# Hash-masked attention with an MLP behind it: values loaded a head at a time over all partitions, one store a unit, first score steps over three pairs of banks

## The chip, the cores and the metric

One Trainium2 chip; the kernel runs on one core of it. The metric is the device time of one execution in microseconds (us), as a median over runs; a profile is of one further execution.

## The reference, cut to what matters

```python
def _attn_ref(q, k, v, proj):            # q, k, v: (4, 8, 768, 64) f32; proj: (64, 6)
    q_bits = (np.einsum('bhsd,dk->bhsk', q, proj) > 0).astype(np.int64)
    k_bits = (np.einsum('bhsd,dk->bhsk', k, proj) > 0).astype(np.int64)
    powers = 2 ** np.arange(n_bits)
    q_bucket = np.sum(q_bits * powers, axis=-1)
    k_bucket = np.sum(k_bits * powers, axis=-1)
    mask = q_bucket[:, :, :, None] == k_bucket[:, :, None, :]
    scores = np.where(mask, scale * np.matmul(q, k.transpose(0, 1, 3, 2)), -1e9)
    attn = softmax(scores)
    return np.matmul(attn, v)

def _moe_ref(x, g_ln, w_ch1, w_ch2):     # x: (4, 768, 512), the heads side by side
    xn = (x - mu) / np.sqrt(var + 1e-06) * g_ln
    ch = np.maximum(xn @ w_ch1, 0.0) @ w_ch2      # 512 -> 2048 -> 512
    return x + ch
```

Each query attends to the keys whose six sign bits equal its own. The result, with the eight heads side by side, goes through a layer norm and a two-layer MLP, and is added to it.

## The kernel before, in words

The work is cut into 12 **units** u of 256 query rows, three for each batch b. A unit has six **score steps** s = 6u + 3g + kp: g is a group of four heads, kp a pair of key blocks (256 keys). The whole program is a list of words, `ORDER`, each `operation.engine.arguments` (v VectorE, a ScalarE, p GpSimd, s SyncE, t TensorE); the kernel goes through it and issues one operation after the other. Each engine executes its own words in that order and waits at a word until its inputs are there and its output's buffer is free. A transfer's words stand in the queue of the engine that issues them in the same way. So a word that waits holds every later word of its engine.

The words that matter here, with lines of the kernel before:

- **Loads of q and k.** `lx` (batch 0) loads the slices of some kp for four heads, `LX` (L417, other batches) 768 KB at once, into one of four buffers X. `gx` is a memset that claims such a buffer ahead of the load.
- **Turning.** `tn`, `tu` (L234) transpose 32x32 blocks on VectorE; `ca`, `CA` (L237 to 245) cast to bf16, as `qb` and `kb`.
- **Hash.** `ha` and `hc` (batch 0) and `hm` multiply by `proj` on TensorE; `bh`, `bc`, `bt` make bits of +0.5 and -0.5 on VectorE. In batch 0 `sl`, `bi` spread `hc`'s bits; in the others `mw` and `mr` (`G<-Bd`, L452) send them through DRAM. The result G lies so that the product of two G blocks is the mask, added to the scores in the same bank.
- **Values.** `lv` loads values into `vn` (two buffers of four heads each), `cv` (L381) casts them into `vaug` (values and a column of ones), two heads a word; `su`, `sp` or `sq`, and `sc` (L411) make their sum over keys, `vsB`.
- **Steps.** `S` (L476) is 24 matmuls into two pairs of PSUM banks (8 with G, 16 with q and k); `E` (L482) is the exponential on ScalarE, one activation of 128x1024 for each pair; `A` (L501) is 16 matmuls of E with the values into `acc`, which sums over the three steps of a group.
- **End of a unit.** `na`, `nb` divide by the row's sum into x; `nc`, `ce` make the layer norm's statistics and the centred rows; `rs` the inverse deviation on GpSimd; `fl` transposes by DMA (for unit 0 `ft` and `fc` do it on TensorE).
- **MLP.** `F` (L558, p = 0 to 7, 16 matmuls each) the first product, `R` (L566, L568) its ReLU, `D` (L574, in quarters, for each of two row tiles) the second product, `Z` (L582) adds x, `O` (L592) stores. `lw1`, `lw2` (L365, L368) load the weights through GpSimd's queue, four pieces each.
- **Dummies.** `warm`, `wm` and `wa` are matmuls on ones whose results are never read; `warm` is the first `NWARM` of them.

PSUM has eight banks: `scA` two, `scB` two, `acc` two, `f1` and `f2` one each. Buffers of one tag are handed out in turn: E has four, X four, vn two.

The first three score steps (`ROT = (2, 1, 0)`) run over three pairs of banks, scA, scB and acc, since no A has begun by then:

```python
tag = ("scA", "scB", "acc")[(2 * ROT.index(s) + h) % 3] if s in ROT else ("scA", "scB")[h]
```

The hash products `hf` of batch 0 lie in f1 and f2 in turn. The rows of a tile are rows of the sequence in the order 24 tt + 6 c + kj (tt = 0 to 31, c = 0 to 3, partition 32 c + tt). In batch 0 the keys are put by `key_order` into the order of a plain load of values, four heads over 128 partitions in one transfer of 768 KB; in the other batches the values are loaded in the order of the keys, by four transfers of 32 partitions each:

```python
if b == 0:
    eng.dma_start(out=vnat(b, hs), in_=v[b, hs : hs + 4].rearrange("h (p kj) d -> p h (kj d)", p=P))
else:
    eng.dma_start(out=vnat(b, hs)[32 * c : 32 * c + 32], in_=v_view[b][c][:, hs : hs + 4])
```

A unit's rows are stored by four transfers of 32 partitions (128 KB) in the same way, the last unit's in 16 smaller ones on SyncE's and ScalarE's queues.

Of the kernel before, what the change touches and what calls it, by code (L numbers as in the profile page):

```python
# [8 lines left out]
F32 = mybir.dt.float32  # L9
# [4 lines left out]
NWARM = 8  # L14

ROT = (2, 1, 0)
# [7 lines left out]
bh.v.0.1.0 tn.v.1.1.1 ca.v.1.1.1 ha.t.1.1.1 cv.p.0.0.0 E.a.1.1 gx.p.1.0.0 LX.s.1.0.0 bh.v.1.1.1 cv.p.0.0.2 S.t.0.2
E.a.0.0 ha.t.1.0.0 tn.v.1.1.0 ha.t.1.1.0 bh.v.1.0.0 S.t.4.2 bh.v.1.1.0 E.a.0.1 ca.p.1.1.0 tn.v.1.0.2 ha.t.1.1.2
bh.v.1.1.2 cv.p.0.4.2 tn.v.0.0.2 lv.s.1.4.3 A.t.1.2 cv.p.0.4.0 E.a.4.0 sq.t.0.0 lw1.p.2 E.a.4.1 lv.s.1.0.3 S.t.3.2
A.t.2.2 lv.s.1.4.0 sc.a.0.0 lw1.p.1 E.a.3.0 tn.v.0.0.1 hc.t.0.0.2 hc.t.0.0.1 bc.v.0.0.1 E.a.3.1 bc.v.0.0.2 sl.t.0.0.1
bi.a.0.0.1 ca.v.0.0.1 tn.v.1.0.1 sl.t.0.0.2 S.t.5.2 ca.p.1.0.1 lv.s.1.4.1 bi.a.0.0.2 E.a.5.0 A.t.0.2 na.v.0.0 nb.v.0.0
nc.v.0.0 sq.t.0.4 E.a.5.1 sc.v.0.4 S.t.8.2 gx.v.1.0.1 E.a.8.0 gx.v.1.1.0 A.t.5.2 A.t.4.2 ca.p.1.0.2 tu.v.1.0.0.0
LX.s.1.0.1 A.t.3.2 E.a.8.1 na.v.0.1 nb.v.0.1 lw1.p.3 S.t.6.2 E.a.6.0 lv.s.1.0.1 nc.v.0.1 ce.v.0.0 hc.t.1.0.2 hc.t.1.0.1  # L30
A.t.8.2 bc.v.1.0.1 E.a.6.1 S.t.7.2 A.t.6.2 bc.v.1.0.2 lv.s.1.4.2 ce.v.0.1 E.a.7.0 pmem.p tu.v.1.0.0.1 rs.p.0 gx.v.1.1.1
sl.t.1.0.1 on.p.1 sl.t.1.0.2 LX.s.1.1.1 bi.v.1.0.2 bi.v.1.0.1 E.a.7.1 lw1.p.0 tu.v.1.0.0.3 ft.t.0.1 ft.t.0.0 fc.v.0.0
LX.s.1.1.0 S.t.9.2 tu.v.1.0.1.2 fc.a.0.1 A.t.7.2 lw2.p.1 lw2.p.0 tu.v.1.0.1.1 lw2.p.3 ca.a.0.0.2 cv.p.1.4.0 F.t.0.4
tu.v.1.0.1.3 E.a.9.0 E.a.9.1 na.v.1.0 F.t.0.3 R.v.0.4 S.t.10.2 R.a.0.3 A.t.9.2 lw2.p.2 E.a.10.1 F.t.0.6 tu.v.1.0.0.2
CA.v.1.0.0 E.a.10.0 nb.v.1.0 nc.v.1.0 R.a.0.6 F.t.0.7 S.t.11.2 E.a.11.0 tu.v.1.0.1.0 E.a.11.1 CA.p.1.0.1 su.p.1.4
hm.t.1.0 bt.v.1.0 A.t.10.2 R.a.0.7 tu.v.1.1.0.2 tu.v.1.1.1.3 tu.v.1.1.1.1 S.t.14.2 tu.v.1.1.0.1 mw.s.1.0 mr.s.1.0.0
F.t.0.2 tu.v.1.1.0.3 R.v.0.2 A.t.11.2 E.a.14.1 na.v.1.1 nb.v.1.1 E.a.14.0 F.t.0.5 tu.v.1.1.1.2 S.t.12.2 R.v.0.5 F.t.0.0
E.a.12.0 nc.v.1.1 R.v.0.0 E.a.12.1 A.t.14.2 F.t.0.1 S.t.13.2 A.t.12.2 R.a.0.1 lv.s.1.0.2 D.t.0.0.0 E.a.13.0 ce.v.1.0
E.a.13.1 D.t.0.0.1 ce.v.1.1 rs.p.1 fl.s.1.1 tu.v.1.1.1.0 fl.s.1.0 tu.v.1.1.0.0 mr.s.1.0.3 S.t.16.2 E.a.16.0 E.a.16.1
LX.s.2.0.0 mr.s.1.0.2 hm.t.1.1 lv.s.1.0.0 bt.v.1.1 CA.p.1.1.0 mr.s.1.0.1 D.t.0.0.2 mw.s.1.1 sp.t.1.4 sc.v.1.4 S.t.15.2  # L40
cv.p.1.4.2 F.t.1.7 R.v.1.7 E.a.15.0 E.a.15.1 cv.p.1.0.0 A.t.13.2 D.t.0.0.3 na.v.2.0 F.t.1.5 CA.a.1.1.1 Z.v.0.0 S.t.17.2
LX.s.2.1.1 E.a.17.1 R.v.1.5 mr.s.1.1.3 su.p.1.0 D.t.0.1.0 F.t.1.2 R.v.1.2 LX.s.2.0.1 mr.s.1.1.1 mr.s.1.1.0 LX.s.3.0.1
D.t.0.1.1 E.a.17.0 S.t.18.2 E.a.18.1 lv.s.2.0.3 mr.s.1.1.2 F.t.1.3 R.v.1.3 D.t.0.1.2 D.t.0.1.3 nb.v.2.0 E.a.18.0
F.t.1.0 lv.s.2.0.0 A.t.15.2 S.t.20.2 E.a.20.0 R.v.1.0 F.t.1.1 R.a.1.1 Z.v.0.1 tu.v.2.0.0.1 A.t.17.2 nc.v.2.0 A.t.16.2
F.t.1.4 cv.p.1.0.2 tu.v.2.0.0.3 E.a.20.1 S.t.19.2 E.a.19.0 na.v.2.1 A.t.20.2 R.v.1.4 nb.v.2.1 nc.v.2.1 ce.v.2.1
lv.s.2.4.1 tu.v.2.0.0.2 D.t.1.0.0 E.a.19.1 fl.s.2.1 F.t.1.6 R.a.1.6 S.t.21.2 D.t.1.0.1 E.a.21.0 E.a.21.1 lv.s.2.4.2
ce.v.2.0 tu.v.2.0.0.0 D.t.1.0.2 D.t.1.0.3 CA.p.2.0.0 tu.v.2.0.1.0 tu.v.2.0.1.1 sp.t.1.0 sc.a.1.0 A.t.18.2 fl.s.2.0
S.t.22.2 E.a.22.1 LX.s.2.1.0 E.a.22.0 tu.v.2.0.1.2 tu.v.2.0.1.3 CA.a.2.0.1 hm.t.2.0 O.s.0.0 lv.s.2.0.1 Z.v.1.0 bt.v.2.0
D.t.1.1.0 S.t.23.2 F.t.2.0 LX.s.3.0.0 E.a.23.1 D.t.1.1.1 lv.s.2.4.3 lv.s.2.4.0 R.a.2.0 E.a.23.0 tu.v.2.1.0.0 lv.s.2.0.2
# [59 lines left out]
def kernel(  # L109
# [16 lines left out]
    P = 128  # L126
# [510 lines left out]
```

## Time and profile before

| what | value |
|---|---|
| runs | 308.54, 305.88, 308.46 us; median 308.46 |
| profiled execution, span | 308.1 us |
| TensorE busy | 297.0 us, 96% of the span |
| ScalarE, VectorE, GpSimd busy | 187.9 (61%), 174.4 (57%), 84.6 us (27%) |
| moved by DMA | 34.32 MB |
| TensorE's first and last matmul | starts at 1.11, last ends at 303.74 us |
| last store landed | 306.4 us |

The profiled execution's span, 308.1 us, lies 0.4 us below the median of the runs and is the yardstick for the working; the time that the runs give is counted as the span and those 0.4 us. A row of a time view gives the start of an instruction, its time, its engine and line, the operation, output and input with partitions and elements, and in brackets the idle time ahead of it with what ended that.

### The profile page before, as it was taken

What the parts mean: (1) busy time and instruction counts of PE and PEld (TensorE: products, weight loads), DVE (VectorE), ACT (ScalarE), POOL (GpSimd) and SP (SyncE); (2) the same over time, 40 slices, a digit from 0 to 9 for tenths busy, and PEclk for the clock granted to TensorE, in tenths of its full rate; (3) what the DMA queues carried; (4) which work ended last, traced back from release to release, by engine and by line L of the source; (5) the groups of instructions that cost most, each with busy time, mean ns of one, the idle gap of its engine ahead of it and who ended that gap; (6) DMA issues with size and microseconds to landing.
All of it is one profiled execution on the core that took longest, in us unless ns stands there. A gap on an engine that the chain in (4) does not pass through costs nothing.

```text
span 308.1 us, 9875 instructions
## 1 busy us (share of the span) xinstructions
PE 297.0 (96%) x4394; PEld 203.9 (66%) x4394; DVE 174.4 (57%) x363; ACT 187.9 (61%) x204; POOL 84.6 (27%) x102
## 2 busy tenths in 40 slices
PE   8898699999999999999999999999999999999994
PEld 4576477567667766856676677676676776676663
DVE  4757777646926956666866434556464335345112
ACT  3687667775786867755657586665755686351220
POOL 3675625626233950141020028301001001001000
PEclk9999779999999999999999999999999999999999
DMA  6999999488594587124032030131010501103032
GB/s 213 358 263 194 296 252 199 69 248 232 118 278 112 135 106 192 46 65 129 2 87 54 9 108 2 40 81 36 10 45 19 102 4 27 43 2 91 30 85 69
DMA packets 31290, 34.32 MB, mean 111 GB/s; under 512 B 15632, under 2 KB 27920, under 8 KB 31248
## 3 DMA queue, kind: packets, MB, share of 16 engines
q1 hardware_dynamic: 26656, 29.24, 37.2%
q0 software_dynamic: 4224, 4.19, 8.4%
q8 instruction: 34, 0.56, 0.8%
q10 hardware_dynamic: 368, 0.26, 0.3%
q14 instruction: 8, 0.07, 0.1%
HBM read 28.12 MB, written 6.88 MB: 114 GB/s over the span
## 4 chain that ended last, share of the span: by engine, by line
PE 86%; DVE 4%; DMA 4%; ACT 3%; SPq 1%; issue 1%; DVEq 0%
PE f L558 27%; PE sc L476 17%; PE acc L501 11%; ACT E L482 3%; DMA X<-in_k_dram 3%; PE hp L431 2%; PE hf L323 1%; DMA xnT<-xc 1%; PE f_60None L574 1%; PE f_11None L574 1%; PE f_31None L574 1%; PE f_71None L574 1%; PE f_50None L574 1%; PE f_21None L574 1%; PE f_20None L574 1%; PE f_101None L574 1%
## 5 line engine op out<-in xcount | busy, mean ns | idle before, releaser
L482 ACT ACTIVATE E<-sc,bias_sb 128x1024 bf16<-128x1024 f32 x144 | 153.5, 1110 | 64.1 <-PE sc L476 64.1
L558 PE MATMUL f<-xnT,w_sb 128*128 128x256 bf16 x768 | 100.6, 275 | 0.2 <-DMA xnT<-xc 0.2
L558 PEld LDWEIGHTS <-w_sb 128*128 128x128 bf16 x768 | 71.9, 98 | 22.1 <-issue 5.2
L568 DVE TENSOR_SCALAR hb<-f 128x512 bf16<-128x512 f32 x48 | 33.0, 688 | 46.9 <-PE f L558 46.3
L574 PEld LDWEIGHTS <-hb 128*128 128x128 bf16 x400 | 36.7, 98 | 33.3 <-issue 4.5
L476 PE MATMUL sc<-qb,kb 32*128 32x256 bf16 x1152 | 53.1, 269 | 0.0
L566 ACT ACTIVATE hb<-f 128x512 bf16<-128x512 f32 x48 | 28.6, 596 | 39.9 <-PE f L558 38.5
L501 PEld LDWEIGHTS <-E 128*128 128x128 bf16 x1152 | 41.8, 98 | 7.4 <-issue 5.1
L501 PE MATMUL acc<-vaug,E 128*128 128x65 bf16 x1152 | 45.7, 195 | 0.0
L476 PE MATMUL sc<-G 6*128 6x256 bf16 (+1 forms) x576 | 43.3, 275 | 1.8 <-ACT E L482 1.7
L536 POOL TENSOR_SCALAR rs<-mv 128x2 f32<-128x2 f32 x12 | 7.8, 654 | 123.2 <-DVE mv L530 122.9
L476 PEld LDWEIGHTS <-kb 32*128 32x128 bf16 x1152 | 30.8, 94 | 1.6
L476 PEld LDWEIGHTS <-G 6*128 6x128 bf16 (+1 forms) x576 | 16.1, 91 | 20.6 <-issue 18.7
L234 DVE STREAM_TRANSPOSE T<-X 128x384 f32<-128x384 f32 x48 | 25.5, 558 | 3.7 <-DMA X<-in_q_dram 3.7
L514 DVE SCALAR_TENSOR_TENSOR y<-vsB,acc 128x520 f32<-128x520 f32 x24 | 16.5, 687 | 18.0 <-PE acc L501 18.0
L531 DVE SCALAR_TENSOR_TENSOR xc<-x,mv,gB 128x512 bf16<-128x512 f32 x24 | 19.1, 798 | 0.9
L381 POOL CAST vaug<-vn 128x768 bf16<-128x768 f32 x16 | 13.5, 859 | 17.8 <-DMA vn<-in_v_dram 11.8
L527 DVE BATCH_NORM_STATS2 st<-x 128x6 f32<-128x256 f32 x48 | 17.6, 411 | 0.3
L389 POOL TENSOR_TENSOR t<-vn 128x768 f32<-128x768 f32 x6 | 10.9, 1814 | 24.7 <-DMA vn<-in_v_dram 24.7
L523 DVE TENSOR_TENSOR x<-y,rc 128x512 f32<-128x512 f32 x24 | 17.2, 715 | 0.8
L243 POOL TENSOR_SCALAR qb<-T 128x1536 bf16<-128x1536 f32 x3 | 12.8, 4267 | 13.5 <-DVE T L234 8.7
L234 DVE STREAM_TRANSPOSE tp<-X 128x256 f32<-128x256 f32 x24 | 9.1, 419 | 3.9 <-DMA X<-in_k_dram 2.8
(115 smaller groups left out, 240.1 us busy)
## 6 DMA issues: line engine op xcount, KB each, us to landing
out_dram<-x SPq DMA_DIRECT2D x44, 128.0 KB
X<-in_k_dram SPq DMA_DIRECT2D x7, 768.0 KB
X<-in_q_dram SPq DMA_DIRECT2D x6, 768.0 KB
vn<-in_v_dram SPq DMA_DIRECT2D x24, 192.0 KB
w_sb<-in_moe_w_ch_dram POOLq DMA_DIRECT2D x8, 512.0 KB, 11.5
vn<-in_v_dram SPq DMA_DIRECT2D x2, 768.0 KB
X<-in_q_dram SPq DMA_DIRECT2D x2, 512.0 KB
Bd<-B SPq DMA_DIRECT2D x6, 96.0 KB
```

Of the source, the lines that this page charges most:

```text
L234: nc.vector.transpose(d[:, j], s[:, j, kj0 : kj0 + n])
L476: nc.tensor.matmul(sc(s, i // 2)[:, i % 2, 256 * kk : 256 * kk + 256], lh, rh, start=(rep == 0), stop=(rep == 2), skip_group_check=True,)
L482: nc.scalar.activation(E(s)[:, heads(h)], sc(s, h), AF.Exp, scale=EXP_SCALE, bias=bias_sb)
L501: nc.tensor.matmul(acc[:, qt, (D + 1) * i : (D + 1) * (i + 1)], E(s)[:, i, 256 * kk + P * qt : 256 * kk + P * qt + P], vaug(u // 3)[:, 4 * ...
L514: nc.vector.scalar_tensor_tensor(yt(u, g), vs, EPS_ROW, made[f"acc{u}{g}"][:, :, :A], op0=AOP.mult, op1=AOP.add,)
L523: nc.vector.tensor_tensor(xo, a[:, :, :, 0:D], rc.to_broadcast([P, 2, 4, D]), op=AOP.mult)
L527: nc.vector.bn_stats(stats(u)[:, qt, g], xt(u)[:, qt, 256 * g : 256 * g + 256])
L531: nc.vector.scalar_tensor_tensor(xc(u)[:, t], xt(u)[:, t], mv(u)[:, t, 0:1], gB, op0=AOP.subtract, op1=AOP.mult,)
L558: nc.tensor.matmul(f1[:, n].rearrange("p (t x) -> p t x", t=2), w1_sb[:, dt, P * nt : P * nt + P], xnT(u)[:, :, dt], start=(dt == 0), stop ...
L566: nc.scalar.activation(hb(u)[:, 2 * p : 2 * p + 2], f1, AF.Relu)
L568: eng.tensor_scalar_max(hb(u)[:, 2 * p : 2 * p + 2], f1, 0.0)
L574: nc.tensor.matmul(f2, hb(u)[:, nt, P * t : P * t + P], w2_sb[:, nt, half(h)], start=(nt == 0), stop=(nt == NNT - 1),)
```

## The change: what it does

Everything is in one step:

- **Values.** `lv` loads one head in one transfer of 192 KB, for all batches: the address list is `c tt (kj d)`, 4 x 32 x 384, onto 128 partitions. `key_order` is dropped: keys of batch 0 stay as loaded. `lv` words: 26 before, 32 after. Some of the `cv` words go to ScalarE and VectorE (10 of 16 stay on GpSimd).
- **Stores.** `O` stores a whole unit in one transfer of 512 KB with the list `c tt (qt d)`, 4 x 32 x 1024; the last unit's goes in three parts. `O` words: 50 on SyncE and 6 on ScalarE before, 14 on SyncE after.
- **Score steps.** The first six (`ROT = (2, 1, 0, 4, 3, 5)`) run over three pairs of banks, and the third pair is now f1 and f2, two tiles of one bank; its E is two activations of 512 in place of one of 1024. The hash products of batch 0 lie mostly in the accumulators' banks.
- **Accumulator.** `acc` is two tiles of one bank; `na` is two instructions in place of one.
- **Small things.** `NWARM` 1 in place of 8; four `wa` words (8 matmuls); `ag` (the statistics' aggregation) a word apart from `ce`; buffers are handed out by an explicit count (`turns`); the load of the activation table moves to a late place.
- **Order.** The whole list of words is remade. It begins with key and query slices and then the eight heads of batch 0's values, one word each.

```diff
-NWARM = 8
-
-ROT = (2, 1, 0)
+NWARM = 1
+
+ROT = (2, 1, 0, 4, 3, 5)
...
-on.p.0 mem.v lp.a tab.a warm.t wm.t.0 wm.t.1 lx.s.0.0.0.1 lx.s.0.1.1.3 pf.v wm.t.2 wm.t.3 lx.s.1.1.0.3 lx.s.0.1.0.1
-lx.s.1.0.0.1 tn.v.0.0.0 ca.a.0.0.0 lx.s.1.0.1.3 lv.s.0.0.4 lv.s.0.4.4 sel.p lx.s.0.0.1.3 p32.p ha.t.0.0.0 wm.t.4 wm.t.5
...
+lx.s.0.1.1.2 mem.v lp.a lx.s.0.0.0.1 wm.t.6 sel.p lx.s.0.1.2.3 wm.t.1 wm.t.0 lx.s.1.0.0.1 wm.t.4 lx.s.0.1.0.1 wm.t.7
+warm.t lx.s.1.1.0.3 pf.v p32.p wm.t.3 lv.s.0.0.2 wm.t.2 tn.v.0.1.1 lv.s.0.0.0 wm.t.5 lv.s.0.0.3 ha.t.0.1.1 ca.p.0.1.1
+tn.v.0.0.0 lv.s.0.4.1 ca.p.0.0.0 ha.t.0.0.0 tn.v.0.1.2 lv.s.0.4.0 bh.v.0.1.1 ca.a.0.1.2 lv.s.0.0.1 bh.v.0.0.0
+ha.t.0.1.2 tn.v.1.0.0 lv.s.0.4.3 tn.v.0.1.0 S.t.1.2 bh.v.0.1.2 ha.t.1.0.0 ca.p.0.1.0 E.a.1.1 ca.v.1.0.0 on.p.0
+lv.s.0.4.2 gx.p.1.0.0 ha.t.0.1.0 E.a.1.0 bh.v.1.0.0 lx.s.0.0.1.3 tn.v.1.1.1 S.t.2.2 LX.s.1.0.0 bh.v.0.1.0 tn.v.1.1.2
...
+D.t.10.1.3 R.a.11.3 F.t.11.5 Z.v.10.1 D.t.11.1.1.1 O.s.10 R.v.11.5 D.t.11.0.0 F.t.11.6 D.t.11.0.1 R.v.11.6
+D.t.11.1.2.1 F.t.11.7 D.t.11.0.2 R.a.11.7 D.t.11.0.3 D.t.11.1.3.1 Z.v.11.0 D.t.11.1.1.0 Z.v.11.1.1 D.t.11.1.2.0
+O.s.11.0 D.t.11.1.3.0 O.s.11.1.1 Z.v.11.1.0 O.s.11.1.0
...
-    v_view = [v[b].rearrange("h (tt c kj) d -> c tt h (kj d)", tt=TT, c=CC) for b in range(B)]
-    out_view = [out[b].rearrange("(tt c u qt) d -> u c tt qt d", tt=TT, c=CC, u=3) for b in range(B)]
+    v_view = [v[b].rearrange("h (tt c kj) d -> h c tt (kj d)", tt=TT, c=CC) for b in range(B)]
+    out_view = [out[b].rearrange("(tt c u qt) d -> u c tt (qt d)", tt=TT, c=CC, u=3) for b in range(B)]
...
+            if tag == "acc":
+                n = turns.get("ps acc", 0)
+                turns["ps acc"] = n + 1
+                tag = f"acc_{n % 2}"
...
-        dst, src = qk(t, 0, g)[:, :, 256 * kp : 256 * kp + 256], tp(g, t, kp)
-        if t == 1:
-            dst = dst.rearrange("p j (n t c) -> p j n t c", c=CC, t=TT)
-            src = src.rearrange("p j (n c t) -> p j n t c", c=CC, t=TT)
-        cast(eng, t, dst, src)
+        cast(eng, t, qk(t, 0, g)[:, :, 256 * kp : 256 * kp + 256], tp(g, t, kp))
...
-        return ps(f"hf{g}{t}{kp}", [P, 512], ("f1", "f2")[(t + kp + g) % 2])
+        return ps(f"hf{g}{t}{kp}", [P, 512], "acc" if t or not kp else ("f1", "f2")[g])
...
-    def lv(eng, b, hs, c):
-        if b == 0:
-            eng.dma_start(out=vnat(b, hs), in_=v[b, hs : hs + 4].rearrange("h (p kj) d -> p h (kj d)", p=P))
+    def lv(eng, b, hs, h):
+        eng.dma_start(out=vnat(b, hs)[:, h], in_=v_view[b][hs + h])
...
-            eng.dma_start(out=vnat(b, hs)[32 * c : 32 * c + 32], in_=v_view[b][c][:, hs : hs + 4])
...
+        if eng is nc.scalar:
+            nc.scalar.copy(dst, src)
         else:
...
+            eng.tensor_copy(dst, src)
...
-        tag = ("scA", "scB", "acc")[(2 * ROT.index(s) + h) % 3] if s in ROT else ("scA", "scB")[h]
-        return ps(f"sc{s}{h}", [P, 2, 512], tag)
+        pair = (2 * ROT.index(s) + h) % 3 if s in ROT else h
+        if pair == 2:
+            return [ps(f"sc{s}.{h}.{n}", [P, 512], ("f1", "f2")[n]) for n in range(2)]
+        t = ps(f"sc{s}{h}", [P, 2, 512], ("scA", "scB")[pair])
+        return [t[:, n] for n in range(2)]
...
     def E_(eng, s, h):
-        nc.scalar.activation(E(s)[:, heads(h)], sc(s, h), AF.Exp, scale=EXP_SCALE, bias=bias_sb)
+        whole = made.get(f"sc{s}{h}")
+        if whole is not None:
+            nc.scalar.activation(E(s)[:, 2 * h : 2 * h + 2], whole, AF.Exp, scale=EXP_SCALE, bias=bias_sb)
+        else:
+            for n in range(2):
+                nc.scalar.activation(E(s)[:, 2 * h + n], sc(s, h)[n], AF.Exp, scale=EXP_SCALE, bias=bias_sb)
...
-    def O_(eng, u, *a):
...
+    def O_(eng, u, t=None, h=None):
+        dst, src = out_view[u // 3][u % 3], xt(u).rearrange("p t d -> p (t d)")
+        if t is not None:
+            c0 = DM * t + (0 if h is None else 256 * h)
+            dst, src = dst[:, :, c0 : c0 + (DM if h is None else 256)], src[:, c0 : c0 + (DM if h is None else 256)]
+        eng.dma_start(out=dst, in_=src)
```

In the new order the key cast `ca.p.1.1.1`, which S.4 reads, comes behind the casts of six heads on GpSimd (heads 2 and 3 are cast on ScalarE ahead of E.2), and the load of k's group 0 of batch 1 (`LX.s.1.0.1`) behind seven of the eight heads of batch 1's values.

More of the change, by code (lines that the diff above doesn't have):

```diff
@@ L24 @@
[L24 to L28, printed above, removed]
@@ L496, in A_ @@
         begun.add((u, g))
-        acc = ps(f"acc{u}{g}", [P, 2, 512], "acc")
+        acc = [ps(f"acc{u}{g}{qt}", [P, 512], "acc") for qt in range(2)]
         for kk in range(2):
```

221 lines of the change are left out of this document (105 added, 116 removed).

## The prediction

> **What bounds the kernel now.** I read the engine totals first, then the slices, then the chain that ended last, then the opening in order of time.
>
> ```profile
> PE 297.0 (96%) x4394; PEld 203.9 (66%) x4394; DVE 174.4 (57%) x363; ACT 187.9 (61%) x204; POOL 84.6 (27%) x102
> PEclk9999779999999999999999999999999999999999
> DMA  6999999488594587124032030131010501103032
> PE 86%; DVE 4%; DMA 4%; ACT 3%; SPq 1%; issue 1%; DVEq 0%
> ```
>
> TensorE is full, and the chain is 86% TensorE. Busy time can be padded, so I laid the starts of the matmuls against the words of the order: a score step S takes 0.77 us to the next word, A 0.49, F 0.87, a quarter D 0.86, and entering an S costs 0.1 more. From S.18 (69.1 us) on, the sum of these is 233.0 us and the measured stretch to the last matmul (303.7) is 234.6. So after 69 us nothing is to be gained but work itself; what can move is the opening, where the DMA row stands at 9, and the stores behind the last matmul.
>
> ```profile
> 9.80 2.12 ACT L482 ACTIVATE E<-sc,bias_sb 128x1024 bf16<-128x1024 f32 x2 [1.55 <-PE sc L476]
> 15.14 0.83 POOL L381 CAST vaug<-vn 128x768 bf16<-128x768 f32 x1 [0.45 <-DMA vn<-in_v_dram]
> 16.70 1.08 POOL L245 CAST kb<-tp 128x512 bf16<-128x512 f32 x1
> 24.14 2.12 ACT L482 ACTIVATE E<-sc,bias_sb 128x1024 bf16<-128x1024 f32 x2 [0.29 <-PE sc L476]
> 27.14 2.12 ACT L482 ACTIVATE E<-sc,bias_sb 128x1024 bf16<-128x1024 f32 x2 [0.89 <-PE sc L476]
> 30.14 2.12 ACT L482 ACTIVATE E<-sc,bias_sb 128x1024 bf16<-128x1024 f32 x2 [0.89 <-PE sc L476]
> 33.09 2.12 ACT L482 ACTIVATE E<-sc,bias_sb 128x1024 bf16<-128x1024 f32 x2 [0.83 <-PE sc L476]
> ```
>
> From 24 to 33 us a step costs 3.0 us: 2.12 of ScalarE, and 0.9 in which it waits for scores that need the banks it has just left. POOL's first cast of values waits 0.45 us for its load; the waits view shows how near POOL keeps to the loads of values:
>
> ```profile
> POOL vaug L381 <- DMA vn<-in_v_dram: 11.8, 3, 10.1
> ```
>
> three waits, 11.8 us, the longest 10.1. The slices show TensorE at 0.7 of its clock around 35 us.
>
> **The loads.** Times of landing are the semaphore events of the trace. The first 2 MB had landed at 11.48 us; then four heads of values (768 KB) landed at 15.08 and the next four at 17.18, so 768 KB over 16 DMA engines, 48 KB on each, took 2.10 us. Not every transfer has 16: the 24 transfers `G<-Bd`, whose address list has 8 outermost rows on one side and 16 on the other, raise their semaphore in 9 steps, all other loads and stores of SP in 16. I read this as one step for the engines that have no part and one for each of 8 that have. The change makes the outermost count 4: a head is now `c tt (kj d)`, c=4 steps of 384 elements outside tt=32 steps of 1536, which do not merge, and the store is `c tt (qt d)` likewise. By the same reading each such transfer has **four engines**. A head of 192 KB then puts 48 KB on each of the four: 2.10 us for one head, where four heads took that. The trace does not tell which four; I take the same four each time, since each issue is alike, and keep the other case as a rival.
>
> The Trainium skill, "DMA: Bandwidth & Descriptors", section on why a DMA increments its semaphore by 16, says that the number of engines is the largest up to 16 that divides the slowest dimension of both sides, and that they are the lowest-numbered ones; the first half agrees with the 9 steps here, the second no run here shows.
>
> **The change part by part.**
>
> *Values, batch 0.* Ahead of them stand the same 2 MB (11.5 us by the row; 8.8 if each engine's packets ran without a gap). Eight heads at 2.10 follow one another: the third lands at 17.8, the sixth at 24.1, the eighth at 28.3. POOL's order is the cast of heads 6 and 7 (0.86), then the key cast ca.1.1.1 (1.07), which S.4 needs: S.4 at 30.4, against 17.1 now. ScalarE has the cast of heads 2 and 3 ahead of E.2 and stands until 17.8; that is covered by the later wait, and would cost about 4 us alone.
>
> *What is queued behind.* On those four engines everything issued later from SP waits: q of group 0 (512 KB, 1.5: 29.8), LX.1.0.0 (768 KB, 2.1: 31.9), q of group 1 (33.4), then seven heads of batch 1 (14.7) and the gain (0.65): 48.7. Weights share the engines; their landings stand 2.5 us apart (47.28, 49.82, 52.41), and four of the eight pieces are issued by POOL ahead of this point: 10 us, 58.7. LX.1.0.1 is next: 60.8, against 37.4 now. VectorE meets tu.1.0.1.1, which reads it, straight after the two copies fc of unit 0, and stands there; behind it are bc.0.0.2 and R.0.3, and TensorE has sl.0.0.2 and hc.1.0.2, which need these two, ahead of S.10. Two transposes 1.0, bc 0.2, R 0.65, hc 0.25 and handovers 0.4 give S.10 at **63.3**, against 42.45. Ends: 57 (loads from 8.8, the last two weight pieces half behind) and 66.
>
> *Six steps over three pairs, hash in the accumulators' banks.* With a third pair the next S runs under the second half of E, so a step falls from 3.0 to about 2.2. Four halves are now two activations of 512 (0.60 each by the ReLU row of that size, against 1.06): 0.5 us. That gain lies in 9 to 38 us and is swallowed by the wait to 63; cover gone, it is worth some 3 us.
>
> *Small edits, at nothing.* Seven first warm matmuls (0.43 each) go from time spent waiting for the first load; without that cover removing them would only gain. Eight wa matmuls (0.11 each) fill TensorE's waits for E, else 0.9. The plain key casts (0.63 on ScalarE against 1.12 in key order) save 0.5 off the path. 24 na in halves cost VectorE about 0.1 each, under its 43% of idle time; ag apart from ce costs nothing.
>
> *The rest.* The same sum of words from S.10 to the last matmul is 259.8 us in the new order (258.9 in the old, which took 261.3; I add the same 2.4). No bank or E is late later on: S steps stand 3.07 us apart or more from S.14 on; from a unit's last A to its first F there are at least 14.8 us (8.7 now). Three places are tighter, all through loads:
> - CA.1.0.0 on POOL stands behind sums that need LX's next neighbour, the last head of batch 1; tu.1.1.0.3 waits for its buffer, R.0.0 behind it holds F.0.4: 3.4 us (0 to 5).
> - From hm.1.1 to S.22 there are 10.7 us (20.0 to the first such S now, of which the chain took 18.3: last G landed at 78.65). With heads of batch 2 on the four engines: 3 us (0 to 6).
> - The clock fell for 6.8 us at 35 us, which cost TensorE 3.1. It will fall again in the longer waits, mostly while nothing is due: 0.6 (0 to 3).
>
> *The tail.* A store of 512 KB puts 128 KB on each of four engines; by X's packets (6144 bytes in 234 ns) 5.0 us, off the path until the last unit. There 256 KB, 128 KB and 128 KB follow one another: 2.6, 1.5 and 1.5 us. They begin 1.65 us after the first issue, 2.1 us before the last matmul's end, and so land 5.3 us behind that end with the semaphore's 0.2, against 2.7 now: +2.6, so 4.3+2.6 = 6.9. Thirty fewer issues of about 0.42 us on SP and six fewer on ACT free queues that wait anyway.
>
> Sum: 63.3+259.8+2.4+3.4+3.0+0.6+6.9 = 339.4. The ends of the first term pull down more than up (its weights may run on under POOL's waits), and I take 3 us off: 336.4 of span. The profiled span of 308.1 stands 0.4 below the median of 308.46, so some **336.5**; own range 324 to 350.
>
> The skill's "TensorE: Matmul & The Clock Gate", Part 1, has the clock halved after an idle window of 3.4 us until a busy one; 6.8 us here are two such windows. By it each long wait (20 to 30 us, 48 to 62 us) would begin the next work at half clock, some 1.7 us each, 3 us in the sum in place of 0.6.
>
> **Rivals.**
> 1. *Sixteen engines after all: faster.* The address lists might be cut anew when the transfer is issued. For it: nothing but G is narrow now, and lists of 512 rows against 128 get 16. Against: G's 9 steps, at 8 against 16. Then values land as now, E runs nearly without a gap from 9.1 us, S.9 comes at 33.3 (37.17 now), and 262.3 of words, 1.5 of waits where S.9, S.10, S.11 and S.14 stand under 3.05 apart, 1.6 of small losses and 1.6 at S.22 follow: 300.3, with a tail of 4.1: 304.4, about 304.8.
> 2. *Four engines, other ones each time.* Four heads then run side by side, 768 KB in about 2.1 us, each only later by 1.6. The opening's gain of 4 us is eaten by that and by the tail: about 308, no change. Nothing in the trace speaks for or against.
> 3. *Only the first wait binds.* If LX.1.0.1 gets past the weights and lands before 48, the delay is S.4's 13.3 us less the 4 that the new banks give back, with a tail of +2.6: about 320. For it: weights lie on all engines, and POOL may issue them later than I say.
>
> **How the numbers follow.** Forecast 0.72, first rival 0.10, second 0.06, third 0.12. Slower by over 1% (which is about what a measurement here can tell from no change) holds the forecast and the third, 0.84; within 1% the second, 0.06; faster by over 1% the first, 0.10. The range leaves out the first two and ends at 314, below the third, and at 350, the upper ends of the single terms not all together.
>
> **What would show it.** Each vn and out transfer should raise its semaphore in five steps; a head should take 2 us and more on its own; POOL's casts of values should wait for vn until near 28 us; S.10 should start near 60; VectorE should show one wait of over 10 us for X of k; the clock should fall in 20 to 62 us; the last store should land over 5 us behind the last matmul. If vn lands in 16 steps, or all eight heads before 18 us, the forecast is wrong at its root; if S.10 comes before 50, the term behind it.

## The result and the profile after

The changed kernel takes **372.73 us** (median of four runs, 370.46 to 374.09), against 308.5 us: slower by a factor of 1.2098 (95% interval 1.2023 to 1.2173). Forecast were 336.5 us in a range of 314 to 350. The direction holds, and so does the mechanism of the loads; the size does not, by 36 us, and the stores, which the forecast held to be off the path, are on it.

The profiled execution has a span of 370.6 us. The first fence is from its page: engine totals, clock, DMA and the shares of the chain that ended last.

```profile
PE 305.5 (82%) x4349; PEld 211.6 (57%) x4395; DVE 182.8 (49%) x393; ACT 188.8 (51%) x209; POOL 71.5 (19%) x95
...
PEclk9955966799996999987998999999999999999997
DMA  7286589489526220594481155052110111901222
...
PE 52%; DMA 26%; DVE 9%; SPq 5%; POOL 3%; issue 2%; POOLq 0%; DVEq 0%
```

The work is the same; TensorE's 297.0 us have become 305.5 because more of it ran at half clock (291.5 in a kernel of the same order but for one word, below, whose clock did not fall while it worked). But its share fell from 96% to 82%, and DMA has 26% of the chain in place of 4%. The next rows are the opening in order of time, where steps had followed each other every 3.0 us before (start, us, engine and line; in brackets the idle time ahead and what ended it).

```profile
17.72 0.83 ACT L378 CAST vaug<-vn 128x768 bf16<-128x768 f32 x1 [5.76 <-DMA vn<-in_v_dram]
18.10 1.92 SPq L311 DMA_DIRECT2D X<-in_q_dram  x1
...
21.83 0.82 POOL L380 CAST vaug<-vn 128x768 bf16<-128x768 f32 x1 [10.88 <-DMA vn<-in_v_dram]
...
24.78 0.83 POOL L380 CAST vaug<-vn 128x768 bf16<-128x768 f32 x1 [2.12 <-DMA vn<-in_v_dram]
...
30.14 0.83 POOL L380 CAST vaug<-vn 128x768 bf16<-128x768 f32 x1 [4.53 <-DMA vn<-in_v_dram]
...
31.58 0.61 PE L475 MATMUL sc<-qb,kb 32*128 32x256 bf16 x8 [2.44 <-POOL kb L254]
...
32.87 2.12 ACT L483 ACTIVATE E<-sc,bias_sb 128x1024 bf16<-128x1024 f32 x2 [9.48 <-PE sc L475]
...
63.12 1.04 DVE L243 STREAM_TRANSPOSE T<-X 128x384 f32<-128x384 f32 x2 [7.83 <-DMA X<-in_k_dram]
```

GpSimd's casts wait for one head after the other until 30 us, S.4's key cast stands behind them, ScalarE gets its scores at 32.87 us after 9.48 us of nothing, and at 63 us VectorE has waited 7.83 us for k of batch 1. The chain in order of time says the same and goes on:

```profile
16.13 13.89 DMA vn<-in_v_dram
31.60 15.13 DMA vn<-in_v_dram
48.12 19.85 DMA vn<-in_v_dram
...
110.79 5.92 DMA G<-Bd
...
159.68 6.26 DMA xnT<-xc
```

Each of the three rows of values is one head of 192 KB, from issue to landing; most of that is standing in a line, not transfer. The landings, read from the semaphore events of the traces:

| transfer | before | after |
|---|---|---|
| steps of the semaphore, values and stores | 16 | 5 |
| third, sixth, eighth head of batch 0 landed | (four at 15.08, eight at 17.18) | 17.70, 24.66, 30.02 |
| k of group 0, batch 1 (`LX.1.0.1`) landed | 37.4 | 63.10 |
| S.10 starts | 42.45 | 66.09 |
| a unit's store, issue to landing | (pieces of 128 KB) | 10.0 to 10.9 for 512 KB, with no other store ahead |
| last matmul's end to the span's end | 4.3 | 9.0 |

And the number of engines at work can be read directly. A row of the windows view has the stretch, its length, each engine's busy time, the clock, the DMA share (of 16 engines) and GB/s. The first is of the changed kernel, where only heads of batch 0 were moving; the second of the kernel with stores in two halves (below), during its last stores.

```profile
14.00:17.50 3.50, 0.26 (x2) 0.09 (x1) 1.27 (x4) 0.00 (x0) 0.00 (x0) 1.00 0.27 97
```

```profile
366.00:376.00 10.00, 0.00 (x0) 0.00 (x0) 0.00 (x0) 0.00 (x0) 0.00 (x0) 0.50 0.13 49
```

0.27 of 16 is 4.3 engines, 0.13 of 16 is 2.1: the outermost counts 4 and 2.

The loads with all 16 engines that stand behind the heads show that the four are the same each time. q of group 0, issued at 18.10 us, raises its semaphore twelve times by 25.31 us and the last four times between 29.57 and 31.42, around and behind the landing of the eighth head (30.02); k of group 0 of batch 1 has its twelve by 52.99 and its last four between 58.58 and 63.10. Twelve engines were free, and four stood in the line.

### The profile page after: what moved, and what is told of

The parts are those of the page before. It is cut to its first block, busy times and chain, and to the rows that moved or that the text cites. A ratio compares the mean times of both kernels' runs of the same rounds, so it can differ in the third digit from the quotient of the medians.

```text
span 370.6 us, 9834 instructions
## 1 busy us (share of the span) xinstructions
PE 305.5 (82%) x4349; PEld 211.6 (57%) x4395; DVE 182.8 (49%) x393; ACT 188.8 (51%) x209; POOL 71.5 (19%) x95
## 4 chain that ended last, share of the span: by engine, by line
PE 52%; DMA 26%; DVE 9%; SPq 5%; POOL 3%; issue 2%; POOLq 0%; DVEq 0%
PE f L565 17%; DMA vn<-in_v_dram 13%; PE sc L475 9%; PE acc L505 6%; DMA out_dram<-x 5%; DMA G<-Bd 4%; SPq L372 3%; DMA Bd<-B 3%; DVE x L528 2%; DMA xnT<-xc 2%; PE hp L427 2%; DVE T L243 2%; DVE hb L575 1%; POOL qb L252 1%; SPq L311 1%
## 5 line engine op out<-in xcount | busy, mean ns | idle before, releaser
L483 ACT ACTIVATE E<-sc,bias_sb 128x1024 bf16<-128x1024 f32 x140 | 149.7, 1111 | 108.7 <-PE sc L475 105.8
L565 PE MATMUL f<-xnT,w_sb 128*128 128x256 bf16 x768 | 102.8, 279 | 10.5 <-DMA xnT<-xc 6.6
L475 PE MATMUL sc<-qb,kb 32*128 32x256 bf16 x1120 | 56.0, 278 | 2.4 <-POOL kb L254 2.4
L505 PEld LDWEIGHTS <-E 128*128 128x128 bf16 x1152 | 45.1, 102 | 8.5 <-issue 4.6
L505 PE MATMUL acc<-vaug,E 128*128 128x65 bf16 x1152 | 48.7, 199 | 0.0
L475 PEld LDWEIGHTS <-kb 32*128 32x128 bf16 x1152 | 31.7, 97 | 4.7 <-POOL kb L254 2.7
L519 DVE SCALAR_TENSOR_TENSOR y<-vsB,acc 128x260 f32<-128x260 f32 x48 | 18.0, 416 | 20.6 <-PE acc L505 20.5
L528 DVE TENSOR_TENSOR x<-y,rc 128x512 f32<-128x512 f32 x24 | 21.6, 901 | 4.9 <-DMA out_dram<-x 4.2
L543 POOL TENSOR_SCALAR rs<-mv 128x2 f32<-128x2 f32 x12 | 4.6, 383 | 100.4 <-DVE x L589 72.3
L385 POOL TENSOR_TENSOR t<-vn 128x768 f32<-128x768 f32 x6 | 11.1, 1851 | 56.1 <-DMA vn<-in_v_dram 56.0
L380 POOL CAST vaug<-vn 128x768 bf16<-128x768 f32 x10 | 8.4, 847 | 69.9 <-PE f L565 38.7
L538 DVE SCALAR_TENSOR_TENSOR xc<-x,mv,gB 128x512 bf16<-128x512 f32 x24 | 18.0, 754 | 5.8 <-DMA gB<-in_moe_g_ln_dram 5.4
```

What stands on the lines that cost most here:

```text
L475: nc.tensor.matmul(sc(s, i // 2)[i % 2][:, 256 * kk : 256 * kk + 256], lh, rh, start=(rep == 0), stop=(rep == 2), skip_group_check=True,)
L483: nc.scalar.activation(E(s)[:, 2 * h : 2 * h + 2], whole, AF.Exp, scale=EXP_SCALE, bias=bias_sb)
L505: nc.tensor.matmul(acc[qt][:, (D + 1) * i : (D + 1) * (i + 1)], E(s)[:, i, 256 * kk + P * qt : 256 * kk + P * qt + P], vaug(u // 3)[:, 4 * ...
L519: nc.vector.scalar_tensor_tensor(yt(u, g)[:, qt], vs, EPS_ROW, made[f"acc{u}{g}{qt}"][:, :A], op0=AOP.mult, op1=AOP.add,)
L528: nc.vector.tensor_tensor(xo, a[:, :, :, 0:D], rc.to_broadcast([P, 2, 4, D]), op=AOP.mult)
L538: nc.vector.scalar_tensor_tensor(xc(u)[:, t], xt(u)[:, t], mv(u)[:, t, 0:1], gB, op0=AOP.subtract, op1=AOP.mult,)
```

## The experiments

All ratios are to the kernel before the change, run on the same chip beside them (medians 307.96 to 308.98 us). "Narrow" is a list with outermost count 4.

| kernel | us | ratio, 95% interval |
|---|---|---|
| changed: values narrow, stores narrow | 372.7 | 1.2098 (1.2023 to 1.2173) |
| values flat | 337.0 | 1.0932 (1.0879 to 1.0986) |
| stores flat | 352.8 | 1.1480 (1.1415 to 1.1546) |
| both flat | 318.6 | 1.0343 (1.0277 to 1.0409) |
| both flat, weight piece earlier | 312.3 | 1.0151 (1.0085 to 1.0217) |
| both flat, wait filled with dummies | 317.1 | 1.0304 (1.0262 to 1.0346) |
| only batch 0's values flat | 359.7 | 1.1665 (1.1590 to 1.1740) |
| values in pieces | 352.6 | 1.1466 (1.1383 to 1.1550) |
| stores in pieces | 358.8 | 1.1683 (1.1599 to 1.1767) |
| both in pieces | 341.3 | 1.1092 (1.1021 to 1.1163) |
| values flat, stores in halves (count 2) | 382.7 | 1.2420 (1.2359 to 1.2480) |
| before, values of batches 1 to 3 narrow | 322.8 | 1.0488 (1.0408 to 1.0569) |
| before, stores narrow | 316.8 | 1.0270 (1.0198 to 1.0343) |
| right results, both flat, weight piece earlier | 317.3 | 1.0299 (1.0227 to 1.0371) |
| before, flat values | 308.1 | 1.0002 (0.9965 to 1.0038) |

**First: is it the lists or the order?** The theory was the forecast's: a narrow list runs on four engines and everything behind it in SP's queue waits. The rival was that the remade order, the banks or the missing dummies cost the time. The first three kernels replace the narrow lists by pieces of 32 partitions (outermost count 32), in the values, in the stores, and in both; the fourth puts narrow lists into the kernel before.

Values in pieces, four transfers at the first word of a group of four heads:

```diff
-        eng.dma_start(out=vnat(b, hs)[:, h], in_=v_view[b][hs + h])
+        if (b, hs) in loaded:
+            return
+        loaded.add((b, hs))
+        for c in range(CC):
+            eng.dma_start(
+                out=vnat(b, hs)[32 * c : 32 * c + 32],
+                in_=v[b, hs : hs + 4].rearrange("h (tt c kj) d -> c tt h (kj d)", tt=TT, c=CC)[c],
+            )
```

> The changed kernel, but the values are loaded in lists whose outermost count is 32: at the first word of a group of four heads four transfers of 32 partitions (192 KB each) are issued, the other three words of the group issue nothing. Stores stay as changed (outermost count 4). Theory 1 (a list with outermost count 4 runs on four engines; the values hold the opening, the stores the middle and the tail): vn raises its semaphore in 16 steps, eight heads of batch 0 land before 18 us, S.10 starts at about 40 us in place of 66.1, the wait at S.22 goes; left are the tail (about 9.7 us behind the last matmul) and the waits behind stores near 160 and 190 us; some 320 us (312 to 330). Rival A (the remade order and the new banks cost the time, the loads are hidden by other waits): no more than 15 us comes back, 357 or above. Rival B (the stores cost nearly all of it): 365 or above.

Measured: 352.56 us, S.10 at 49.41. Between the two theories: 20 us came back, not 53.

Stores in pieces:

```diff
-        eng.dma_start(out=dst, in_=src)
+        for c in range(CC):
+            eng.dma_start(out=dst[c], in_=src[32 * c : 32 * c + 32])
```

> The changed kernel, but each store word issues four transfers of 32 partitions (outermost count 32) in place of one with outermost count 4. Values stay as changed. Theory 1: S.10 stays at 66 us; the tail behind the last matmul falls from 9.7 to about 3.5 us; the waits that stand behind stores (F.3.7 near 160 us with 6.6 us, S.39 near 190 us with 3.1 us, and the half clock behind each, some 3 us) go in part: some 352 us (345 to 360). Rival A (order and banks): only the tail comes back, 366. Rival B (the stores cost nearly all): 330 or below.

Measured: 358.84 us, inside theory 1's range and 7 us above its figure; S.10 at 64.90. The waits at F.3.7 and S.39 are gone. The time behind the last matmul fell only to 7.3 us, not to 3.5: the last unit's pieces are now twelve transfers, issued one after the other.

Both edits:

> The changed kernel with values and stores both in lists of outermost count 32 (the edits of the two kernels before this one together); order, banks, dummies and buffers as changed. Theory 1: everything that was lost comes back, S.10 at about 40 us, no wait of over 3 us on TensorE after it: 304 to 312 us, as before the change or a little faster. Rival A (the remade order, the six steps over three pairs of banks, or the missing first dummies cost the time): 330 or above.

Measured: 341.34 us, S.10 at 50.04. By the letter the rival wins: 33 us of loss are left with 16 engines on every transfer. But the trace shows a second reason. Batch 0's pieces landed at 13.87, 14.85, 15.65 and 16.67 us, almost 1 us for each 192 KB, where the 768 KB in one transfer over 128 partitions had taken 2.10; and there are four times as many issues where a store stands. The substitute was not a neutral one.

Narrow lists in the kernel before, in batches 1 to 3, nothing else changed:

```diff
-            eng.dma_start(out=vnat(b, hs)[32 * c : 32 * c + 32], in_=v_view[b][c][:, hs : hs + 4])
+            eng.dma_start(out=vnat(b, hs)[:, c], in_=v[b, hs + c].rearrange("(tt c kj) d -> c tt (kj d)", tt=TT, c=CC))
```

> The kernel before the change in everything but one line: for batches 1 to 3 the transfer of a group's 32 partitions (outermost count 32) is replaced by the transfer of one head over 128 partitions with outermost count 4; the same number of transfers and bytes at the same words. Batch 0 as before. Theory 1: each of the 24 transfers takes 2.0 us on four engines; five of them stand ahead of the load of k for batch 1, which lands some 8 us later than 37.4, so S.10 comes some 6 us later, and single waits follow later on: some 320 us (312 to 332). Rival A (the form of the list costs nothing by itself, the new order does): within 1% of 308.

Measured: 322.79 us, near the figure of theory 1, but not at its place, so that the agreement is partly luck: S.10 came at 38.52, earlier than the 42.45 of before, and the time went later, to waits of 4.6 us ahead of F.0.0 at 53 us and of 3.3 us ahead of the sums of batch 2 at 111 us, with slow words behind them. So the list costs 14 us even in the old order, and its form alone is enough.

**Second: the same transfers, with another outermost count.** To leave everything but the count as it was, the next kernels load and store rows in plain order: the same words, bytes, packets and partitions, but 128 outermost rows on both sides ("flat").

```diff
-        eng.dma_start(out=vnat(b, hs)[:, h], in_=v_view[b][hs + h])
+        eng.dma_start(out=vnat(b, hs)[:, h], in_=v[b, hs + h].rearrange("(p kj) d -> p (kj d)", p=P))
...
-    out_view = [out[b].rearrange("(tt c u qt) d -> u c tt (qt d)", tt=TT, c=CC, u=3) for b in range(B)]
+    out_view = [out[b].rearrange("(u p qt) d -> u p (qt d)", u=3, p=P) for b in range(B)]
```

> The changed kernel with the same transfers at the same words (one a head, one a unit, same bytes, same packets of 1536 and 4096 bytes, all 128 partitions), but with rows in plain order, so that the outermost count is 128 on both sides: values as (p kj) d -> p (kj d), stores as (u p qt) d -> u p (qt d). What is changed in the computation: value rows no longer stand beside their keys, and output rows are permuted. Theory 2 (after the runs with transfers in pieces: the lists cost some 31 us, and the remade order some 25 to 33 us more, because loads stand behind store words in SP's queue and transposes behind bulk loads): vn and out in 16 steps, a head in about 0.55 us, and still waits at D.0.0.1, D.2.0.0 and S.32; some 330 us (320 to 341). Rival C (what was left of the loss with wide pieces, 341 us, came from four times as many issues and from pieces of 32 partitions, which took 0.95 us for 192 KB): 303 to 315.

Measured: **318.64 us**, in neither range: 4 us above rival C's upper end and 1 us below theory 2's lower end. Values and stores raise their semaphore in 16 steps, a head takes 0.50 us, the eighth lands at 16.00, S.10 starts at 39.65, earlier than before the change, and the time behind the last matmul is 3.2 us (4.3 before). The count alone is worth 372.7 - 318.6 = 54 us of the 64; the pieces had cost some 23 us of their own.

With only the values flat:

> The values in plain order as in the kernel before this one (value rows no longer beside their keys), the stores as changed (outermost count 4). Theory 2: the narrow stores cost some 11 us beside wide values (352.6 against 341.3 in pieces), half of it in the tail: some 341 us if the kernel with both takes 330. Rival C: about 315 to 325.

Measured: 336.97 us, between the two. Narrow stores cost 18.3 us beside flat values.

Narrow stores in the kernel before:

```diff
+            stored[u] = stored.get(u, 0) + 1
+            if stored[u] == 4:
+                whole = out[u // 3].rearrange("(tt c u qt) d -> u c tt (qt d)", tt=TT, c=CC, u=3)
+                eng.dma_start(out=whole[u % 3], in_=xt(u).rearrange("p t d -> p (t d)"))
+            return
```

> The kernel before the change in all but the stores of units 0 to 10: at the last of a unit's four store words one transfer of 512 KB with outermost count 4 is issued, the other three words issue nothing; the last unit is stored as before. Theory 1: each store takes some 10 us on four engines (5 us if its 128 packets ran without a gap) and what is issued behind it waits: some 316 us (310 to 325), the tail as before or up to 5 us later if unit 10's store is still under way. Rival D (stores are hidden in this order): within 1% of 308.

Measured: 316.84 us, as theory 1 had it, but most of it in the tail, 6.8 us where theory 1 had at most 5: the last matmul ends at 305.16, the span at 316.3, so 11.1 us in place of 4.3. The last unit's pieces stood behind narrow stores still under way.

Values flat, a store as two transfers of 64 partitions, outermost count 2:

```diff
+        for c in range(2):
+            eng.dma_start(out=dst[2 * c : 2 * c + 2], in_=src[64 * c : 64 * c + 64])
```

> The changed kernel with values in plain order (value rows no longer beside their keys) and each store word as two transfers of 64 partitions, list 2 x 32 x 1024, outermost count 2. Theory 1 (the outermost count is the number of engines, and they are the same ones each time): 3 steps, two engines busy, 256 KB in some 10 us, a unit's store in 20 us, so transposes behind it come up to 20 us later: 20 to 40 us more than with one transfer of outermost count 4, some 370 us (350 to 390). Rival E (the number of engines follows from the partitions or bytes): no slower than with one transfer, 345 or below.

Measured: 382.73 us, 46 more than with count 4; 3 steps each; the second half of a unit lands 13 to 15 us after its issue in the first nine units; 0.13 of 16 engines busy (shown above). Rival E is out: with 32, 64 and 128 partitions in these runs the number of engines followed the outermost count, and the halves do not go to different engines, since in those units the second lands 5 to 7 us behind the first.

**Third: what is left, 10 us, looked for in the order.** In the flat kernel TensorE stands 5.3 us ahead of F.1.1, by the page. GpSimd's rows around it:

```profile
47.08 0.80 POOL L365 DMA_DIRECT2D w_sb<-in_moe_w_ch_dram  x1
54.35 0.78 POOL L543 TENSOR_SCALAR rs<-mv 128x2 f32<-128x2 f32 x1 [6.47 <-DVE mv L535]
55.21 0.73 POOL L544 TENSOR_TENSOR rs<-rs,mhalf 128x2 f32<-128x2 f32 x1
55.90 0.81 POOL L365 DMA_DIRECT2D w_sb<-in_moe_w_ch_dram  x1
```

The last piece of the weights stands behind `rs.p.1`, which waits 6.47 us for statistics; it is issued at 55.90 and lands at 64.4, and the transpose `fl.1.0`, issued at 56.88, lands at 65.22. One word moved:

```diff
-S.t.13.2 lv.s.2.0.0 ag.v.1.0 ce.v.1.0 rs.p.1 A.t.12.2 E.a.13.1 R.v.0.7 fl.s.1.0 F.t.0.4 tu.v.1.1.1.1 E.a.13.0 lw2.p.3
+S.t.13.2 lv.s.2.0.0 ag.v.1.0 ce.v.1.0 lw2.p.3 rs.p.1 A.t.12.2 E.a.13.1 R.v.0.7 fl.s.1.0 F.t.0.4 tu.v.1.1.1.1 E.a.13.0
```

> The kernel with both lists in plain order (318.6 us; value rows not beside their keys, output rows permuted), with one word of the order moved: the last piece of the weights, lw2.p.3, ahead of rs.p.1 on GpSimd, which waits until 54.35 us for statistics. Theory 3 (the order's own loss is one place: the piece is issued at 55.90 and lands at 64.4, the transpose fl.1.0 behind it lands at 65.22, TensorE stands 5.8 us at F.1.1 and then runs some 3 us slower at half clock): the piece is issued near 48 and fl.1.0 lands near 60, so 6 to 9 us come back: some 311 us (308 to 314). Rival F (the loss is spread over the order, the next wait takes this one's place): 316 or above.

Measured: 312.34 us; `fl.1.0` lands at 57.20, the wait and the half clock behind it are gone. Theory 3 holds for 6.3 of the 10 us. The 4 us that remain were not tried one by one; the longest wait is 2.1 us at 107 us, ahead of the sums of batch 2 (`sp.2.0`). Two rows of this kernel, on GpSimd and on VectorE, say where it comes from:

```profile
103.05 4.09 POOL L252 TENSOR_SCALAR qb<-T 128x1536 bf16<-128x1536 f32 x1 [11.18 <-DVE T L243]
104.22 2.58 DVE L528 TENSOR_TENSOR x<-y,rc 128x512 f32<-128x512 f32 x1
```

The second is `nb`, which takes 0.69 us at the median. It took 2.6 to 3.4 us at the three places of this kernel, and 2.7 and 3.2 us at the two of the changed one, where it began while GpSimd's cast of queries `CA` (4.1 us) was running, and each time it ended 0.3 us ahead of the cast's end. In the kernel before no `nb` began inside that cast; one that began 0.04 us ahead of it took 0.69. Here the slow `nb` holds the ReLU R.2.6 on VectorE, and that holds `sp.2.0`. The wait is there in the changed kernel too (2.7 us at 149 us), so it belongs to the order and not to the lists; no run moved the cast away.

Only batch 0's values flat:

```diff
+        src = v[b, hs + h].rearrange("(p kj) d -> p (kj d)", p=P) if b == 0 else v_view[b][hs + h]
+        eng.dma_start(out=vnat(b, hs)[:, h], in_=src)
```

> The changed kernel with only batch 0's values in plain order (16 engines; value rows of batch 0 not beside their keys); batches 1 to 3 and the stores with outermost count 4. Theory 1 (the transfers on the four engines stand in one line, and S.10 waits for k of batch 1 at its end): the line is 8 x 1.5 = 12 us shorter, the load of k lands some 10 to 14 us before 63.1, S.10 near 54 in place of 66.1, later waits stay: some 361 us (355 to 366). Rival H (the second wait, on the load of k behind batch 1's values, does not move since the SP queue and the buffers hold those loads): 368 or above.

Measured: 359.68 us, S.10 at 52.11, as theory 1 had it: the transfers stand in one line.

Only the stores flat:

> The changed kernel with only the stores in plain order (u p qt) d -> u p (qt d), outermost count 128 (output rows permuted); the values with outermost count 4. Theory 1, the two losses add up: flat stores took 337.0 to 318.6 beside flat values, 18.4 us; so 372.7 less 18.4, some 354 us (350 to 358). Rival J (with narrow values TensorE waits for these anyway, and the stores' waits lie under theirs): 360 or above.

Measured: 352.78 us. The stores cost 20.0 us beside narrow values and 18.3 beside flat ones, the values 35.8 and 34.1: the two losses add up.

**Fourth: the clock behind a wait.** Twenty-four `wa` words ahead of F.1.1 in the flat kernel:

> The kernel with both lists in plain order (318.6 us; value rows not beside their keys, output rows permuted), and 24 wa words (48 matmuls on ones, never read) ahead of F.1.1, where TensorE stood idle from 59.5 to 65.3 us and then ran at half clock until near 72. Theory 4 (the half clock comes from the idle stretch): no half clock behind the wait, the words from F.1.1 to F.1.2 cost some 3 us less, the wait itself stays: some 315.5 us (314 to 317.5). Rival I (the half clock has another cause, or comes anyway): 318 or above.

Measured: 317.05 us against 318.64; the intervals of the two ratios overlap, so the total does not settle it. The stretch does. The windows view, first of the flat kernel, then of the filled one (the clock is the third column from the right; F.1.1 starts at 65.33 in the first and at 63.44 in the second):

```profile
58.90:65.30 6.40, 1.19 (x6) 0.34 (x4) 4.23 (x4) 1.61 (x2) 4.15 (x2) 0.93 1.23 144
65.30:72.00 6.70, 6.42 (x59) 3.98 (x60) 3.85 (x5) 2.12 (x2) 3.32 (x3) 0.55 0.71 241
```

```profile
58.90:65.30 6.40, 6.40 (x79) 5.36 (x77) 3.40 (x4) 0.00 (x0) 2.48 (x1) 1.00 1.17 160
65.30:72.00 6.70, 6.62 (x113) 4.11 (x114) 2.59 (x5) 4.78 (x6) 3.83 (x3) 1.00 0.44 166
```

From the start of F.1.1 to the start of S.17 the flat kernel takes 6.84 us, the filled one 4.09: 2.75 us, as expected. Idle for 5.3 us, TensorE ran its next words at 0.55 of the clock; kept busy with nothing useful, it ran them at 1.00.

**Fifth: is there a version that beats both?** If the transposes of q and k write their columns four apart, partition p holds rows 6p + kj of the sequence, and the flat lists give the reference's results:

```diff
-        d = dst.rearrange("p j (kj c t) -> p j kj c t", c=CC, t=32)
+        d = dst.rearrange("p j (kj t c) -> p j kj c t", c=CC, t=32)
```

> The same as the kernel before this one, but computing the reference: the 32x32 transposes of q and k write their columns four apart (kj t c in place of kj c t), so that partition p holds rows 6p + kj of the sequence, values and stores keep plain lists with outermost count 128, and keys, values and output agree. Theory 3: as the kernel before it if a transpose with columns four apart takes what it took (558 ns for 128x384), some 311 us; rival G: strided columns make the transposes dearer; at twice the time 48 of them cost VectorE 27 us, off the path after the opening, some 5 us in all, 316.

Measured: 317.30 us, rival G. The transposes by shape, in the kernel with flat lists and the piece moved, and in this one (busy us, mean ns):

```profile
L243 DVE STREAM_TRANSPOSE T<-X 128x384 f32<-128x384 f32 x48 | 25.2, 554 | 0.0
```

```profile
L243 DVE STREAM_TRANSPOSE T<-X 128x384 f32<-128x384 f32 x48 | 38.3, 861 | 0.3 <-DMA X<-in_q_dram 0.3
```

The strided columns make them dearer by 55%. That these 13 us of VectorE are what the 5 us came from was not taken apart. The same transposes and flat values in the kernel before:

> The kernel before the change with transposes that write columns four apart, so that key_order and its strided casts fall away in batch 0, and values of batches 1 to 3 loaded one head a transfer in plain order (128 outermost rows, 16 engines) in place of 32 partitions of four heads; stores in quarters as before. It computes the reference. Theory: the key casts cost 0.63 in place of 1.12 us in the opening and a head lands in 0.5 us; TensorE is full after 69 us, so little moves: 306 us (303 to 309). Rival G (strided transposes cost more): 310 or above.

Measured: 308.07 us, ratio 1.0002 (0.9965 to 1.0038): no change, with the transposes as dear as above (867 ns). No version here beats the kernel before.

## Why the prediction was right in direction and wrong in size

**Right.** Outermost count 4 is four engines, the same four each time: five steps of the semaphore, 4.3 engines busy, one head after the other 2.04 us apart (13.62, 15.66, 17.70, 19.75), and the same four steps late in the loads behind them. The Trainium skill, "DMA: Bandwidth & Descriptors", section on why a DMA increments its semaphore by 16, says the same of the count, and that the remaining 16 - k are written at once: steps of 5, 9 and 3 for 4, 8 and 2 engines agree, and the first step comes 0.4 us behind the issue, long before the data. Which engines these are no run here shows.

The opening came within 3 us: eighth head 30.0 (28.3 forecast), S.4 got its keys at 31.6 (30.4), k of batch 1 at 63.1 (60.8), S.10 at 66.1 (63.3). The 3 us that the forecast took off at the end, because the first term was to come earlier, went the wrong way. VectorE's wait for k was 7.8 us and not over 10. (The forecast's last step, 336.4 and 0.4, gives 336.8 and not 336.5.) Below, the forecast's sum against the profile:

| term | forecast | measured |
|---|---|---|
| to S.10 | 63.3, less 3 taken off at the end | 66.1 |
| S.10 to the last matmul: words, old losses | 259.8 + 2.4 | 259.8 + 2.4, taken over |
| the same: new losses, the rest | 3.4 + 3.0 + 0.6 | 33.3 |
| behind the last matmul | 6.9 | 9.0 |
| span | 336.4 | 370.6 |

The words' sum is not measured here but taken over. In the kernel with flat lists and the piece moved, whose clock did not fall, the stretch from S.10 took 267.7 us against these 262.2. So 26.3 of the 34 us that the span is off lie in the new losses of the middle (words against their usual time in the trace):

| place | forecast | measured |
|---|---|---|
| F.0.4, at 81 us | 3.4 | 3.5 |
| S.22, at 107 to 118 us | 3 | 9.4 |
| D.2.0.0, at 148 us | none | 3.0 |
| F.3.7, at 159 to 166 us | none | 6.6 |
| S.39, at 190 to 194 us | none | 3.1 |
| slow words behind these and behind S.10, small waits | 0.6 | some 8 |

Two lines of the waits view show the two longest kinds of wait among these (us in total, times, longest):

```profile
PE sc L475 <- DMA G<-Bd: 11.0, 4, 5.9
PE f L565 <- DMA xnT<-xc: 6.6, 1, 6.6
```

The experiments cut the 36 us another way, by taking things out. The forecast's own figure for this kernel with 16 engines was rival 1, 304.8, so it had the narrow lists at 31.7 us: 2.8 for the stores (their tail, 6.9 against 4.1) and 28.9 for the values. Measured are 54.1 us for the lists, 18.3 to 20.0 for the stores and 34.1 to 35.8 for the values; the rest is the kernel with flat lists, 318.6 in place of 304.8. So 22 of the 36 us are lists, two thirds or more of them stores, and 14 are the order and the other edits. The two cuts need not agree place by place: the wait at F.1.1 of the flat kernel does not stand in the changed one.

**The step that failed first** is the store: "5.0 us, off the path until the last unit". Both halves were wrong. It takes 10 us from issue to landing. The price of 5.0 is 32 packets of 4096 bytes on each engine at 0.16 us without a gap, taken from the loads' packets of 6144 bytes. The stores' packets did take 0.16 us at the median, but 0.23 on the average and up to 0.9, and in most stores two of the four engines ended some 2 us behind the other two: 8.5 to 9.3 us from the first packet to the last, and 1.2 us ahead of the first. The trace of before had stores' packets too, 0.25 us at the median in its tail. And it is on the path, because what stands behind it on those four engines is urgent. `fl.3.0` and `fl.3.1`, issued at 154.15 and 159.68, landed at 165.46 and 165.94, behind the store of unit 1 (landed 156.99), two loads of 768 KB (158.85, 160.93) and two heads (162.89, 164.91): that is F.3.7's wait of 6.6 us and the chain's row of 6.26. `mr.2.1.0`, issued at 187.32 behind the store of unit 2, landed at 194.42: S.39. The forecast's list of tighter places said "all through loads"; transposes and hash bits behind stores were not walked through. That it is the stores is shown: with flat stores both waits are gone (352.8 us, values narrow), and with flat values and narrow stores they stand there, 4.8 and 3.2 us (337.0 us). The tail belongs here too. The last unit's three stores followed one another in 3.2, 1.3 and 1.4 us, near the 2.6, 1.5 and 1.5 forecast, but behind the store of unit 10, which landed at 363.80, 2.2 us behind the last matmul (361.64); hence 9.0 and not 6.9.

**Second, S.22.** The step had the right mechanism and a third of its size: the bits were written (`mw.1.1`) at 98.05 and landed at 107.44, behind four heads of batch 2 (the last at 105.31) and a load (107.17); read back, `mr.1.1.2` and `mr.1.1.3` landed at 116.71 and 116.51 behind another head (116.13). So 9.4 us came of the 3 forecast, above its upper bound of 6. With flat values this wait is gone.

**Third, the clock.** The forecast put 0.6 us on it, with the argument that it falls while nothing is due. The trace has half clock at 17.5 to 38.0, 48.2 to 58.5, 61.9 to 68.7, 113.1 to 119.9, 164.3 to 171.1 and 195.0 to 198.4 us: five begin in a long wait and outlast it, the sixth begins 0.6 us behind one. Of this, work stood in 14 us behind S.10 (2.6, 3.2, 5.0 and 3.4), which at half clock is 7 us lost. That the next work starts slow is what the Trainium skill's "TensorE: Matmul & The Clock Gate", Part 1, has (half after an idle window of 3.4 us, until a busy one): these stretches are multiples of 3.41 us. The sixth stands behind a wait of only 3.0 us, and in the flat kernel one of 3.41 us stands behind a wait of 2.1. The 3 us that the forecast worked out by that page were nearer than its own 0.6, and still less than half of the 7.

**Fourth, the order.** With 16 engines on every transfer the prediction had the order and the other edits as a gain (rival 1, 304.8 against 308.5); the flat kernel took 318.6. S.9 came at 36.69 and not 33.3; the wait behind the weights, with its slow words some 8 us, was not seen, nor the slow `nb` beside GpSimd's cast, which is also the 3.0 us at D.2.0.0 above. Rival 2 (other engines each time) and rival 3 (only the first wait binds) are out by the line of heads and by S.10.

## What to carry to other kernels

Count the outermost dimension of each transfer's list on both sides before counting bytes: where it was 2, 4 or 8 here, it was the number of engines. A transfer of few engines costs its length in time to what is issued behind it on them, and 16-engine transfers behind it wait as well, for their share on those few. Price a transfer from rows of its own direction and packet size, by their mean and not their best, and walk each queue for what is urgent behind it, not only for the transfer itself. When a substitute is to isolate one property of a transfer, keep words, bytes, packets and partitions the same; pieces that "only" restore the engines cost 23 us here of their own. And price a long wait of TensorE with the slow work behind it: in the changed and the flat kernel half clock stood behind every wait of over 5 us (2.75 us where it was filled), and behind two of the four of 2 to 3 us that began at full clock.

## What the runs showed of the hardware that was not expected

- From the fifth narrow head on, the issue of a transfer itself took SP 1.8 to 1.9 us (0.3 to 0.7 for most when flat), and 4.6 us at 33 and 38 us. Five of these issues in a row, from 14.1 to 22.0 us, ended 0.3 to 0.5 us after the landing of the transfer five before them, as if the queue held back its issuer; so wide loads behind were issued later too.
- 192 KB onto 32 partitions with 16 engines took almost 1 us, the same onto 128 partitions 0.50.
- A 32x32 transpose of 128x384 with output columns four apart took 861 ns in place of 554.
- VectorE's product of 128x512 (`nb`) took 2.6 to 3.5 us in place of 0.69 where it began during GpSimd's cast of 128x1536 (4.1 us).
